# Eight LayerNorm tiles of a transformer block turned by DMA instead of by TensorE

## The chip, the cores and the metric

The kernel runs on one core of one Trainium2 chip. The metric is the device time of one execution in microseconds. The kernel before the change took 1726.68 us as the median of three runs, which lay between 1725.7 and 1727.48 us.

## The reference

One block with adaptive LayerNorm: attention over cached keys and values, then a gated feed-forward network (FFN). There are 2048 rows of width 512, 32 query heads and 8 key/value heads of width 128, a window of the last W = 512 keys, and F = 1792.

```python
mod = (_silu(c) @ w_mod).reshape(c.shape[0], 6, 1, -1)
sa, ca, ga, sb, cb, gb = (mod[:, 0], mod[:, 1], mod[:, 2], mod[:, 3], mod[:, 4], mod[:, 5])
h = _layernorm(x, axis=-1) * (1 + ca) + sa
x = x + ga * _A_ref(h, A_k_cache, A_v_cache, A_wq, A_wo)    # q = h@wq; softmax(q k^T / sqrt(128)) v; @wo
h = _layernorm(x, axis=-1) * (1 + cb) + sb
x = x + gb * _B_ref(h, B_w_gate, B_w_up, B_w_down)          # (gelu(h@w_gate) * (h@w_up)) @ w_down
return x
```

All inputs and the output are float32.

## The kernel before

**Arithmetic.** Products keep float32 accuracy with 16-bit matmuls: each factor is split into a high and a low fp16 half, and `mm3` (L87, its matmuls recorded at L91) makes three matmuls of every product. The projections use schemes with seven block products in place of eight (tiles `b`, `t`, `s`, `u`, `x`, and PSUM tiles `qa`, `qb`, `qc`).

**Order of the work.** The rows are worked in two halves of 1024. Attention makes 512 score tiles of 128 queries by 512 keys. One pass of the loop at L1581 is one **tick**, and it emits the instructions of every engine in the order in which the engine will run them:

- `scores(t)` (L989): three matmuls into PSUM tile `ps`. There are only two `ps` banks, so `scores(t+2)` has to wait until `ee` of tick t has been read from its bank.
- `peak(t)` (L998): VectorE takes the negated row maximum `nm` (L1000). `expo(t)` (L1003): ScalarE makes `ee` = exp(ps + nm) (L1009).
- `high(t-2)` (L1019): ScalarE writes the fp16 high half `p` (L1021). `low(t-3)` (L1024): VectorE writes the low half (L1026), and SyncE (SP) issues a DMA transpose of both halves into `pt` (L1030).
- Three tasks from a list for TensorE: PV products `po`, output projection `py`, query projection of later units (`qa`, `qb`, `qc`).
- The planned steps of this tick: first `run(t)`, then loads, then `run(("w", t))`.

All DMAs that matter here are issued by SP in program order (L97 records plain ones). ScalarE (ACT), VectorE (DVE) and GpSimd (POOL) also run strictly in program order, so a waiting instruction holds up all that stands behind it. Work that is planned with `sched` gets a load into the `raw` ring of five buffers, at a tick that a small planner (L1509) takes from the tick at which the buffer's last holder ends.

**The part that is changed.** While the first half's attention runs, the second half's first LayerNorm is made: `plan_gen(1, ...)` (L1211) lays eight tiles of 128 rows, one per 16 ticks, beginning at ticks 78, 94, ... 190. `ln_tile` (L490) gives the steps of one tile, at these ticks after its begin:

- `load`: DMA of 128 rows of x into a `raw` buffer, here called `xs`.
- `stat` (+0, L502): mean and variance on DVE, then a power on POOL (`rs`, L404). `norm` (+3, L506): DVE subtracts the mean and scales, in place (L509).
- `turn` (+5, L511): four TensorE transposes of 128x128 float32 into one PSUM bank `pln` (L514).
- `affine` (+6 and +7, L516): four ScalarE instructions read `pln`, apply scale and shift per feature, and write `hf` (L522). A DMA then keeps `hf` in DRAM (`hs`).
- `parts` (+8 and +9, L527): ScalarE makes fp16 high halves `b` (L534), POOL the low halves (L536). Tiles 0 to 3 make two blocks, tiles 4 to 7 one.

A third set of such tiles (generation 2, later) uses the same function and stays as it is. Where ticks 186 to 190 make `wo` weights, POOL runs four sets of three instructions (`raw`, `wo`, `wo`; L663, L161, L162) in a row, and behind them the chain `lw`, `lu`, `lt` of the next weight's scale (L237, L241, L263), for which DVE's reciprocal `lr` (L267) waits.

**A model for the new instructions.** At the end of the FFN the kernel already turns float32 tiles by DMA: `yt_turn` (L1728) has ScalarE part the 16-bit halves of each word (`yu`, L1733) and SP issue a DMA transpose (`yv`, L1738); `yt_row` joins the halves on ScalarE (L1757) or POOL (L1753).

Of the kernel before, what the change touches and what calls it, by code (L numbers as in the profile page):

```python
# [12 lines left out]
U16 = mybir.dt.uint16  # L13
BF16 = mybir.dt.bfloat16
AF = mybir.ActivationFunctionType
# [3 lines left out]
P = 128  # L19
S, D, F = 2048, 512, 1792  # L20
HQ, HKV, DH = 32, 8, 128
W = 512
KT = D // P
# [3 lines left out]
QT = QB // P  # L27
# [15 lines left out]
NOT = 12  # L43
# [10 lines left out]
NE = 6  # L54
# [5 lines left out]
SETPOS = (20, 14, 13, 12, 10, 8)  # L60
SETPOS2 = (18, 12, 11, 10, 9, 7)
TAIL = 12


@with_exitstack
def block_kernel(ctx: ExitStack, tc: tile.TileContext, x, kT, v, wq, wo, wg, wu, wd, cT, wc, wm, out):
    nc = tc.nc

    const = ctx.enter_context(tc.tile_pool(name="const", bufs=1))
    pool = ctx.enter_context(tc.tile_pool(name="pool", bufs=2))  # L70
# [7 lines left out]
    def raw(name):  # L78
        return pool.tile([P, 512], F32, tag="raw", name=name, bufs=NRAW)
# [4 lines left out]
    def bank(tag, name, bufs):  # L84
        return psum.tile([P, 512], F32, tag=tag, name=name, bufs=bufs)
# [9 lines left out]
    def dma(out_, in_):  # L95
        moved[0] += 1
        nc.sync.dma_start(out_, in_)  # L97
# [5 lines left out]
    def rows_of(t, i):  # L103
        return t[i * P:(i + 1) * P, :]
# [284 lines left out]
    def ln_cols(key):  # L389
        return (1, 0) if key == "a" else (4, 3)  # L390
# [12 lines left out]
    def ln_power(st):  # L403
        nc.gpsimd.tensor_tensor(st["rs"], st["rs"], nhalf, op=ALU.pow)  # L404
# [85 lines left out]
    def ln_tile(gen, i, src):  # L490
        jsc, jsh = ln_cols("a" if gen < 2 else "f")
        qb, i = divmod(i % (2 * QT), QT)
        st = {}

        def load():
            if gen == 2:
                st["x"] = src()
            else:
                st["x"] = raw("xs")
                dma(st["x"], src())  # L500

        def stat():  # L502
            ln_stat(st["x"], st)
            ln_power(st)

        def norm():  # L506
            if gen == 2:
                return pool_ts(st["x"], st["x"], st["mv"][:, 0:1], st["rs"], ALU.subtract, ALU.mult)
            nc.vector.tensor_scalar(st["x"], st["x"], st["mv"][:, 0:1], st["rs"], op0=ALU.subtract, op1=ALU.mult)  # L509

        def turn():  # L511
            st["ps"] = bank("acc", "pln", NACC)
            for dt in range(KT):
                nc.tensor.transpose(st["ps"][:, dt * P:(dt + 1) * P], st["x"][:, dt * P:(dt + 1) * P], ident)  # L514

        def affine(dts):  # L516
            if 0 in dts:
                st["f"] = raw("hf") if gen == 2 else tmp("hf")
            f = st["f"]
            for dt in dts:  # L520
                sl = slice(dt * P, (dt + 1) * P)
                nc.scalar.activation(f[:, sl], st["ps"][:, sl], AF.Identity,  # L522
                                     scale=cols[:, jsc, dt:dt + 1], bias=cols[:, jsh, dt:dt + 1])
            if KT - 1 in dts:
                dma(spilled(gen, qb)[:, :, i * P:(i + 1) * P], f.rearrange("p (k q) -> p k q", k=KT))

        def parts(act):  # L527
            o = slice(i * P, (i + 1) * P)
            f = st["f"].rearrange("p (k q) -> p k q", k=KT)
            for h, name in enumerate(("b11", "b21") if qb == 0 else (None, "b22")):  # L530
                if name:
                    t, src = block(gen, name), f[:, 2 * h:2 * h + 2, :]
                    if act:
                        nc.scalar.activation(t[:, 0:2, o], src, AF.Copy)  # L534
                    else:
                        nc.gpsimd.tensor_tensor(t[:, 2:4, o], src, t[:, 0:2, o], op=ALU.subtract)  # L536

        more = [lambda: parts(True), lambda: parts(False)]
        return load, [stat, norm, turn, lambda: affine((0, 1)), lambda: affine((2, 3))] + more

    TURN = {}

# [79 lines left out]
    def sched(pos, ld, *more, kind="raw", ahead=AHEAD):  # L622
        loads.append(((pos,) + more, ld, kind, ahead))
# [121 lines left out]
    def at(key, *fns):  # L745
        later.setdefault(key, []).extend(fns)
# [464 lines left out]
    def plan_gen(gen, t_ln, t_cb, dcb, src):  # L1211
        for i in range(2 * QT):
            t = t_ln[i]
            load, steps = ln_tile(gen, i, lambda i=i: src(i))
            sched(t, (load, steps[:3]), t + 3, t + 5)
            for off, fn in zip((6, 7, 8, 9), steps[3:]):
                at(("w", t + off), fn)
        for p in range(2):
            sched_combos(gen, p, t_cb + dcb * p)

    plan_gen(1, [78 + 16 * i for i in range(8)], 201, 33, lambda i: rows_of(x, 2 * QT + i))
    for p in range(2):
        sched_combos(2, p, 478 + 10 * p)

# [10 lines left out]
    for g in range(NG):  # L1235
# [6 lines left out]
        if 0 < g < GW:  # L1242
            a, b = plain_steps(g, by)
            sched_pair(g, srcs, t0 - (19 if g > 1 else 13), spread, [(t0 - (12 if g > 1 else 8), a)], [(t0 - (8 if g > 1 else 7), b)])
        elif g >= GW and (not half or pr < GW):
            sched_set(g, srcs, t0, by, spread)
            if not half:
                a, b, c, d, e, f = SETPOS2 if g == GW else SETPOS
# [11 lines left out]
        else:  # L1260
            if g > 0:
                if pr % 2 == 0:
                    load, stat, spread_, parts = k_items(pr)
                    sched(t0 - (22 if g > 2 else 20), (load, [stat]))
                    at(("w", t0 - (19 if g > 2 else 17)), spread_)
                load, stat, spread_, parts = k_items(pr)
                sched(t0 - (7 if g > 2 else 4 if g > 1 else 6), (load, [parts if g != 2 else lambda parts=parts: soon(parts(True))]))
                at(t0 - (3 if g > 2 else 1 if g > 1 else 2), lambda pr=pr: store(("k", pr), KV[0, pr, 0]))
                if pr % 2 == 0:
                    load, stat, spread_, parts = v_items(qd)  # L1270
# [221 lines left out]
    for n in range(NP):  # L1492
        b = T // 2 + 30 + 27 * n
# [84 lines left out]
    with tc.manual_schedule():  # L1578
        begin()
        nexty, invs = [], {}  # L1580
        for t in range(T + TAIL):  # L1581
            now[0] = t
            u, s = divmod(t, 4)
# [83 lines left out]
    for i, q in enumerate((16, 19, 22, 26, 30, 33, 36, 40)):  # L1667
        load, norm, split, turn = ln_turned(i)
# [192 lines left out]
```

## Time and profile before

| | |
|---|---|
| median of the runs | 1726.68 us (1725.7 to 1727.48) |
| span of the profiled execution | 1724.3 us |
| PE (TensorE) busy | 1705.4 us, 99% |
| DVE busy | 1424.2 us, 83% |
| ACT busy | 1257.4 us, 73% |
| POOL busy | 1088.1 us, 63% |
| chain that ended last | PE 92%, ACT 4%, DVE 2%, DMA 2% |

The page gives one time for the profiled execution, its span; it lies 2.4 us below the median of the runs. Busy is the time in which an engine ran at least one instruction. The chain that ended last is followed backwards from the last instruction through whatever each one waited for. The clock that TensorE was granted shows 9 tenths or more in each of the 40 slices of the page.

### The profile page before, as it was taken

The page shows a single profiled execution, that of the slowest core. Times are in us where ns is not written, and L with a number is a line of the kernel's source. Part 1 is how long each engine was busy: PE and PEld are TensorE (multiplying, and loading weights), DVE is VectorE, ACT ScalarE, POOL GpSimd, SP SyncE. Part 2 cuts the span into 40 slices and gives each one's busy share as a digit, 9 for nine tenths or more (in the row PEclk, how much of TensorE's full clock was granted, in tenths as well). Part 3 has the DMA queues.
Part 4 walks back from the last instruction along what each step waited for, and adds up shares of the span by engine and source line. Part 5 has one row for each costly group of instructions (what it writes and reads, how often), then busy time and mean ns, then how long its engine had stood idle before and what let it go on. Part 6 is the DMA issues. An engine that isn't in the chain of part 4 may idle for free.

```text
span 1724.3 us, 26250 instructions
## 1 busy us (share of the span) xinstructions
PE 1705.4 (99%) x7961; PEld 780.0 (45%) x7961; DVE 1424.2 (83%) x2480; ACT 1257.4 (73%) x2823; POOL 1088.1 (63%) x1322
## 2 busy tenths in 40 slices
PE   7999999999999999999999999999999999999999
PEld 4344444444444444444444444444444444444444
DVE  8888888888888999888888888888896788676666
ACT  7988788888878877888778777788785354455442
POOL 3879777776788884655665755757760345735424
PEclk9999999999999999999999999999999999999999
DMA  7999999999999998999999999899997556365353
GB/s 242 222 207 214 214 217 205 226 202 227 213 217 236 201 212 181 212 211 225 216 220 222 211 227 206 198 236 212 222 232 162 164 144 195 121 165 174 99 158 102
DMA packets 693454, 343.51 MB, mean 199 GB/s; under 512 B 579136, under 2 KB 602688, under 8 KB 693312
## 3 DMA queue, kind: packets, MB, share of 16 engines
q1 hardware_dynamic: 693024, 341.30, 85.3%
q8 instruction: 63, 1.03, 0.3%
q14 instruction: 79, 0.65, 0.1%
q10 hardware_dynamic: 288, 0.52, 0.1%
HBM read 137.50 MB, written 63.70 MB: 117 GB/s over the span
## 4 chain that ended last, share of the span: by engine, by line
PE 92%; ACT 4%; DVE 2%; DMA 2%; issue 1%; SPq 0%; ACTq 0%; DVEq 0%
PE py L91 20%; PE po L91 18%; PE ps L91 17%; PE fa L91 8%; PE qa L91 8%; PE fc L91 4%; PE qc L91 4%; PE ya L91 4%; PE qb L91 2%; PE fb L91 2%; PE yc L91 2%; ACT ee L1009 1%; ACT p L1021 1%; PE yb L91 1%; DMA rw<-in_wq 1%
## 5 line engine op out<-in xcount | busy, mean ns | idle before, releaser
L1009 ACT ACTIVATE ee<-ps,nm 128x512 f32<-128x512 f32 x512 | 349.7, 683 | 185.3 <-DVE nm L1000 182.7
L1026 DVE SCALAR_TENSOR_TENSOR p<-ee,rr,p 128x512 f16<-128x512 f32 x512 | 454.4, 888 | 8.5 <-ACT p L1021 8.0
L1000 DVE TENSOR_REDUCE nm<-ps 128x1 f32<-128x512 f32 x512 | 350.1, 684 | 96.8 <-PE ps L91 94.9
L91 PE MATMUL ps<-k,qt 128*128 128x512 f16 x1536 | 414.7, 379 | 4.4 <-ACT ee L1009 3.3
L1021 ACT ACTIVATE p<-ee,rr 128x512 f16<-128x512 f32 x512 | 363.9, 711 | 16.5 <-DVE rr L1017 11.8
L91 PE MATMUL po<-pt,v 128*128 128x512 f16 x1536 | 372.9, 379 | 2.1 <-DMA pt<-p 0.8
L91 PE MATMUL py<-wo,ot 128*128 128x512 f16 x1536 | 371.3, 379 | 0.0
L91 PEld LDWEIGHTS <-w 128*128 128x128 f16 x2184 | 213.4, 98 | 259.6 <-issue 2.0
L91 PEld LDWEIGHTS <-v 128*128 128x128 f16 x1536 | 149.8, 98 | 184.6 <-issue 3.0
L91 PEld LDWEIGHTS <-ot 128*128 128x128 f16 x1536 | 150.3, 98 | 181.2
L91 PEld LDWEIGHTS <-qt 128*128 128x128 f16 x1536 | 145.7, 98 | 178.0 <-issue 6.0
L1337 POOL TENSOR_TENSOR fg<-fg 128x512 f32<-128x512 f32 x48 | 62.9, 1311 | 135.8 <-DVE fg L1311 133.0
L754 DVE SCALAR_TENSOR_TENSOR ot<-po,ot 128x512 f16<-128x512 f32 x128 | 87.8, 686 | 40.4 <-ACT ot L753 39.9
L1321 ACT ACTIVATE at<-fg 128x512 f16<-128x512 f32 x92 | 56.3, 626 | 77.8 <-DVE fg L1311 61.0
L1009 ACT ACTIVATION_READ_ACCUMULATOR ee<-ps,nm 128x1 f32 x512 | 100.1, 196 | 0.0
L970 DVE SCALAR_TENSOR_TENSOR acc<-py,ysc,acc 128x512 f32<-128x512 f32 x128 | 94.7, 739 | 5.3 <-PE py L91 5.3
L91 PE MATMUL qa<-t,w 128*128 128x512 f16 x348 | 84.9, 379 | 0.0
L91 PE MATMUL fa<-t,w 128*128 128x512 f16 x336 | 81.7, 379 | 0.1
L237 POOL TENSOR_TENSOR lw<-lw,half__86 128x1 f32<-128x1 f32 x38 | 25.9, 681 | 85.7 <-DVE lw L188 85.6
L753 ACT ACTIVATE ot<-po 128x512 f16<-128x512 f32 x128 | 73.9, 578 | 5.0 <-PE po L91 5.0
L404 POOL TENSOR_TENSOR rs<-rs,nhalf 128x1 f32<-128x1 f32 x32 | 18.5, 577 | 93.7 <-DVE rs L398 85.8
L91 PEld LDWEIGHTS <-wo 128*128 128x128 f16 x504 | 49.3, 98 | 59.7 <-issue 0.5
(258 smaller groups left out, 2802.9 us busy)
## 6 DMA issues: line engine op xcount, KB each, us to landing
w<-kept SPq DMA_DIRECT2D x123, 256.0 KB, 3.3
wo<-kept SPq DMA_DIRECT2D x72, 256.0 KB, 3.2
kept<-stage SPq DMA_DIRECT2D x67, 256.0 KB, 3.0
raw<-in_wo SPq DMA_DIRECT2D x56, 256.0 KB, 3.2
kept<-w SPq DMA_DIRECT2D x39, 256.0 KB, 3.0
rw<-in_wq SPq DMA_DIRECT2D x38, 256.0 KB, 3.1
hs<-hf SPq DMA_DIRECT2D x32, 256.0 KB, 2.9
pt<-p SPq DMA_TRANSPOSE x512, 3.4
```

Of the source, the lines that this page charges most:

```text
L91: nc.tensor.matmul(ps, a, b, start=first and n == 0, stop=last and n == 2, skip_group_check=chain)
L237: nc.gpsimd.tensor_tensor(out, out, half_, op=ALU.pow)
L404: nc.gpsimd.tensor_tensor(st["rs"], st["rs"], nhalf, op=ALU.pow)
L753: nc.scalar.activation(t[:, 0, :], src, AF.Copy, scale=scale)
L754: return lambda: nc.vector.scalar_tensor_tensor(t[:, 1, :], src, scale, t[:, 0, :], op0=ALU.mult, op1=ALU.subtract)
L970: nc.vector.scalar_tensor_tensor(acc[ti], st["p"], by, acc[ti], op0=ALU.mult, op1=ALU.add)
L1000: nc.vector.tensor_reduce(nm, E[t]["ps"], axis=AX.X, op=ALU.max, negate=True)
L1009: nc.scalar.activation(e, E[t]["ps"], AF.Exp, bias=E[t]["nm"], scale=1.0, accum_out=sm[:, t % 2:t % 2 + 1])
L1021: nc.scalar.activation(p16[:, 0, :], E[t]["e"], AF.Copy, scale=E[t]["r"])
L1026: nc.vector.scalar_tensor_tensor(p16[:, 1, :], E[t]["e"], E[t]["r"], p16[:, 0, :], op0=ALU.mult, op1=ALU.subtract)
L1321: nc.scalar.activation(t[:, 0, :], g, AF.Copy)
L1337: nc.gpsimd.tensor_tensor(g[o], g[a], g[b], op=ALU.subtract)
```

## The change

For generation 1 (`TG = (1,)`) `turn` is replaced by three steps, and all steps of a tile move into the planner's list, so that the `raw` buffer is held from load to the last step:

- `split` (+4): ScalarE copies `xs` as 16-bit words into `xu`, high halves and low halves apart.
- `spin` (+5): SP issues one DMA transpose of the 128x1024 16-bit words into `xt`.
- `join` (+7): ScalarE interleaves the halves back into the `raw` buffer `xs`, which is float32 again, now turned.
- `affine` (all four at +10) works in place on `xs` in SBUF; there is no `hf` and no PSUM bank.
- `parts` at +11 (ScalarE) and +12 (POOL). Tile 2 and tile 6 begin two ticks later than before, tile 7 one earlier.

```diff
--- before.py
+++ after.py
@@ -60,6 +60,7 @@
 SETPOS = (20, 14, 13, 12, 10, 8)
 SETPOS2 = (18, 12, 11, 10, 9, 7)
 TAIL = 12
+TG = (1,)
 
 
 @with_exitstack
@@ -513,8 +514,21 @@
             for dt in range(KT):
                 nc.tensor.transpose(st["ps"][:, dt * P:(dt + 1) * P], st["x"][:, dt * P:(dt + 1) * P], ident)
 
+        def split():
+            st["u"] = pool.tile([P, 2, W], U16, tag="e", name="xu", bufs=NE)
+            nc.scalar.activation(st["u"], st["x"].bitcast(U16).rearrange("p (r h) -> p h r", h=2), AF.Copy)
+
+        def spin():
+            st["t"] = pool.tile([P, 2 * KT, P], U16, tag="ot", name="xt", bufs=NOT)
+            nc.sync.dma_start_transpose(st["t"], st.pop("u").rearrange("p a b -> p (a b)"))
+
+        def join():
+            a, b = st["x"].bitcast(U16).rearrange("p (q h) -> p h q", h=2), st.pop("t").rearrange("p (h k) q -> p h (k q)", h=2)
+            nc.scalar.activation(a, b, AF.Copy)
+            st["f"] = st["ps"] = st["x"]
+
         def affine(dts):
-            if 0 in dts:
+            if 0 in dts and "f" not in st:
                 st["f"] = raw("hf") if gen == 2 else tmp("hf")
             f = st["f"]
             for dt in dts:
@@ -536,7 +550,7 @@
                         nc.gpsimd.tensor_tensor(t[:, 2:4, o], src, t[:, 0:2, o], op=ALU.subtract)
 
         more = [lambda: parts(True), lambda: parts(False)]
-        return load, [stat, norm, turn, lambda: affine((0, 1)), lambda: affine((2, 3))] + more
+        return load, [stat, norm] + ([split, spin, join] if gen in TG else [turn]) + [lambda: affine((0, 1)), lambda: affine((2, 3))] + more
 
     TURN = {}
 
@@ -1212,13 +1226,11 @@
         for i in range(2 * QT):
             t = t_ln[i]
             load, steps = ln_tile(gen, i, lambda i=i: src(i))
-            sched(t, (load, steps[:3]), t + 3, t + 5)
-            for off, fn in zip((6, 7, 8, 9), steps[3:]):
-                at(("w", t + off), fn)
+            sched(t, (load, steps[:9]), *[t + off for off in (3, 4, 5, 7, 10, 10, 11, 12)])
         for p in range(2):
             sched_combos(gen, p, t_cb + dcb * p)
 
-    plan_gen(1, [78 + 16 * i for i in range(8)], 201, 33, lambda i: rows_of(x, 2 * QT + i))
+    plan_gen(1, [78 + 16 * i + (0, 0, 2, 0, 0, 0, 2, -1)[i] for i in range(8)], 201, 33, lambda i: rows_of(x, 2 * QT + i))
     for p in range(2):
         sched_combos(2, p, 478 + 10 * p)
```

What moves, by engine. On TensorE 32 transposes go and every other row keeps its place.

**ScalarE, around the first tile.** `junk` belongs to another tensor's spread of values. Before:

```order
324 L220 ACTIVATE junk,lm<-raw 128x512
325 L1009 ACTIVATE ee,sm<-ps,nm 128x512
326 L1021 ACTIVATE p_3082<-ee,rr 128x512
327 L522 ACTIVATE hf<-pln,cols 128x128 x2
328 L1009 ACTIVATE ee,sm<-ps,nm 128x512
329 L1014 ACTIVATE rr<-sm 128x2
330 L1021 ACTIVATE p_3116<-ee,rr 128x512
331 L753 ACTIVATE qt<-qd,qsc 128x512
332 L522 ACTIVATE hf<-pln,cols 128x128 x2
333 L1009 ACTIVATE ee,sm<-ps,nm 128x512
334 L1021 ACTIVATE p_3147<-ee,rr 128x512
335 L903 ACTIVATE s_3156<-qa 128x512
```

With the change, the same stretch at three places (`split`, `join`, `affine`):

```order
319 L519 ACTIVATE xu<-xs 128x1024
320 L221 ACTIVATE junk,lm<-raw 128x512
321 L1023 ACTIVATE ee,sm<-ps,nm 128x512
322 L1028 ACTIVATE rr<-sm 128x2
323 L1035 ACTIVATE p_3052<-ee,rr 128x512
324 L767 ACTIVATE ot<-po 128x512
```

```order
329 L1028 ACTIVATE rr<-sm 128x2
330 L1035 ACTIVATE p_3112<-ee,rr 128x512
331 L767 ACTIVATE qt<-qd,qsc 128x512
332 L527 ACTIVATE xs<-xt 128x2x512
333 L1023 ACTIVATE ee,sm<-ps,nm 128x512
334 L1035 ACTIVATE p_3140<-ee,rr 128x512
```

```order
340 L1023 ACTIVATE ee,sm<-ps,nm 128x512
341 L1035 ACTIVATE p_3209<-ee,rr 128x512
342 L536 ACTIVATE xs<-xs,cols 128x128 x4
343 L1023 ACTIVATE ee,sm<-ps,nm 128x512
344 L1028 ACTIVATE rr<-sm 128x2
```

The split stands ahead of a `junk`; the join stands where the second pair of `affine` stood; the four `affine` instructions stand together, three score tiles later, ahead of one `ee`.

**SP, around the first tile.** Before:

```order
178 L1030 DMA_TRANSPOSE pt<-p_3019 128x8x128
179 L97 DMA kept<-wo 128x1024
180 L1030 DMA_TRANSPOSE pt<-p_3050 128x8x128
181 L97 DMA kept<-wo 128x1024
182 L1030 DMA_TRANSPOSE pt<-p_3082 128x8x128
183 L97 DMA hs_0_3131<-hf 512x1x128
```

With the change:

```order
178 L1044 DMA_TRANSPOSE pt<-p_3019 128x8x128
179 L523 DMA_TRANSPOSE xt<-xu 128x8x128
180 L98 DMA kept<-wo 128x1024
181 L1044 DMA_TRANSPOSE pt<-p_3052 128x8x128
182 L98 DMA kept<-wo 128x1024
```

The new transpose goes in directly behind one `pt` transpose and ahead of a plain DMA; the write of `hs` follows later.

**POOL, around ticks 186 to 194.** `b` is the low half of tile 6 (its row before stands 18 rows earlier, at 456); `rs` is tile 7's. Before:

```order
474 L663 TENSOR_TENSOR raw<-raw,gs 128x512
475 L161 TENSOR_SCALAR wo<-raw 128x512
476 L162 TENSOR_TENSOR wo<-raw,wo 128x512
477 L663 TENSOR_TENSOR raw<-raw,gs 128x512
478 L161 TENSOR_SCALAR wo<-raw 128x512
479 L162 TENSOR_TENSOR wo<-raw,wo 128x512
480 L404 TENSOR_TENSOR rs<-rs,nhalf 128x1
481 L237 TENSOR_TENSOR lw<-lw,half__86 128x1
482 L241 TENSOR_SCALAR lw<-lw 128x1
```

With the change:

```order
468 L162 TENSOR_SCALAR wo<-raw 128x512
469 L163 TENSOR_TENSOR wo<-raw,wo 128x512
470 L550 TENSOR_TENSOR b_5426<-xs,b_5426 128x2x128
471 L677 TENSOR_TENSOR raw<-raw,gs 128x512
472 L162 TENSOR_SCALAR wo<-raw 128x512
473 L163 TENSOR_TENSOR wo<-raw,wo 128x512
474 L677 TENSOR_TENSOR raw<-raw,gs 128x512
475 L162 TENSOR_SCALAR wo<-raw 128x512
476 L163 TENSOR_TENSOR wo<-raw,wo 128x512
477 L405 TENSOR_TENSOR rs<-rs,nhalf 128x1
478 L677 TENSOR_TENSOR raw<-raw,gs 128x512
479 L162 TENSOR_SCALAR wo<-raw 128x512
```

Tile 6's `b` now stands among the four `wo` sets, so it lies between them and the `lw` chain behind them; tile 7's `rs` moves ahead of the fourth set.

## Rows read from the trace of the kernel before

**Rows 1.** Busy time by stretch: PE, PEld, DVE, ACT, POOL (instructions), clock, DMA share, GB/s.
```profile
220.00:300.00 80.00, 80.00 (x381) 36.87 (x379) 71.05 (x130) 67.47 (x165) 60.49 (x81) 1.00 0.95 215
...
400.00:520.00 120.00, 120.00 (x571) 55.26 (x570) 103.59 (x190) 97.27 (x235) 94.78 (x123) 1.00 0.97 213
```

**Rows 2.** Chain of waits between 200 and 560 us, by line.
```profile
by line: PE ps L91 25.7%; PE py L91 25.6%; PE po L91 25.5%; PE qa L91 12.6%; PE qc L91 6.5%; PE qb L91 3.2%; PE pln L514 1.0%; PE pst L224 0.0%
```

**Rows 3.** Timeline of PE around the first tile's transposes: start, us, instruction.
```profile
230.66 0.60 PE L514 MATMUL pln<-ident,xs 128*128 128x128 f32 x4
231.10 0.81 PE L91 MATMUL ps<-k,qt 128*128 128x512 f16 x3
...
241.49 0.81 PE L91 MATMUL ps<-k,qt 128*128 128x512 f16 x3
```

**Rows 4.** Tile pln: count, ns min/median/max, first and last start.
```profile
L514 PE MATMUL pln<-ident,xs x32: 272/273/273, 230.7 to 515.5; 128*128 128x128 f32 x32
```

**Rows 5.** Timeline of ACT in the same place (idle before it, and its releaser, in brackets).
```profile
231.24 0.69 ACT L1009 ACTIVATE ee<-ps,nm 128x512 f32<-128x512 f32 x1 [0.41 <-DVE nm L1000]
...
237.93 0.79 ACT L522 ACTIVATE hf<-pln,cols 128x128 f32<-128x128 f32 x2
238.61 0.69 ACT L1009 ACTIVATE ee<-ps,nm 128x512 f32<-128x512 f32 x1
```

**Rows 6.** Groups by line and shape, whole span: busy us, mean ns, idle before, releaser.
```profile
L1733 ACT ACTIVATE yu<-yt 128x1024 uint16<-128x1024 uint16 x16 | 16.5, 1046 | 0.9 <-DVE yt L1707 0.9
...
L1757 ACT ACTIVATE yr<-yv 128x1024 uint16<-128x1024 uint16 x8 | 9.0, 1164 | 1.0 <-DMA out_y<-yr 1.0
...
L553 ACT ACTIVATE xs<-xs,kinv,kmax 128x512 f32<-128x512 f32 x8 | 6.4, 801 | 0.0
...
L448 ACT ACTIVATE hf<-pln,cols 128x512 f32<-128x512 f32 x4 | 2.8, 769 | 0.0
```

**Rows 7.** Groups by line and shape between 220 and 540 us.
```profile
L1009 ACT ACTIVATE ee<-ps,nm 128x512 f32<-128x512 f32 x125 | 85.4, 683 | 41.3 <-DVE nm L1000 40.2 <-POOL w L162 0.4
```

**Rows 8.** Tile pt: issue on SP's queue, who waited for it, landing after issue.
```profile
L1030 SPq DMA_TRANSPOSE pt<-p x512: 1231/1234/3518, 35.5 to 1323.0; - x171
...
  PE po L91: 0.8, 1
...
DMA to landing us min/median/max: 3.0/3.4/6.5
```

**Rows 9.** SP's queue around the first tile's turn.
```profile
233.53 1.29 SPq L1030 DMA_TRANSPOSE pt<-p  x1
234.88 0.57 SPq L97 DMA_DIRECT2D kept<-wo  x1
```

**Rows 10.** Timeline of POOL, 485 to 516 us.
```profile
485.33 1.12 POOL L536 TENSOR_TENSOR b<-hf,b 128x256 f16<-128x256 f32 x1
486.54 0.23 POOL L241 TENSOR_SCALAR ysc<-ysc 128x1 f32<-128x1 f32 x1
...
515.19 0.60 POOL L241 TENSOR_SCALAR lt<-lt 128x1 f32<-128x1 f32 x1
```

**Rows 11.** Timeline of DVE, 515 to 517 us.
```profile
515.82 0.16 DVE L267 RECIPROCAL lr<-lt 128x1 f32<-128x1 f32 x1
...
516.55 0.68 DVE L1000 TENSOR_REDUCE nm<-ps 128x1 f32<-128x512 f32 x1
```

**Rows 12.** Timeline of ACT, 517 and 529 us.
```profile
517.27 0.69 ACT L1009 ACTIVATE ee<-ps,nm 128x512 f32<-128x512 f32 x1 [1.47 <-DVE nm L1000]
...
529.04 0.68 ACT L1009 ACTIVATE ee<-ps,nm 128x512 f32<-128x512 f32 x1
```

**Rows 13.** Timeline of PE, 518 and 531 us.
```profile
518.21 0.81 PE L91 MATMUL ps<-k,qt 128*128 128x512 f16 x3
...
531.16 0.81 PE L91 MATMUL ps<-k,qt 128*128 128x512 f16 x3
```

**Rows 14.** Timeline of PE, 730 to 770 us: waits of over 0.15 us before a score matmul.
```profile
734.36 0.81 PE L91 MATMUL ps<-k,qt 128*128 128x512 f16 x3 [0.19 <-ACT ee L1009]
...
763.76 0.81 PE L91 MATMUL ps<-k,qt 128*128 128x512 f16 x3 [0.16 <-ACT ee L1009]
```

## The prediction

> **What bounds the kernel now.** I read the busy time by stretch first: in the part of the program that the change touches, PE is busy for the whole of each stretch (80.00 of 80 us, 120.00 of 120) at a granted clock of 1.00, while ACT is busy for 84 and 81% of them [rows 1]. The chain of waits through 200 to 560 us then shows what ends last: PE's own instructions and nothing else, the transposes `pln` with 1.0% among them [rows 2]. So in this part the time is the sum of what PE is given to do. An instruction that leaves PE gives back its own length; one that is added elsewhere costs nothing until it makes PE wait.
>
> **What the change takes from PE.** The four transposes of the first tile start at 230.66 us and the score matmuls behind them at 231.10 [rows 3]: 0.44 us. The row of the tile gives 273 ns for one transpose [rows 4], but that is a duration, and pipelined matmuls overlap; what counts is start to start, 0.11 us each. There are 32 transposes [rows 4], in eight tiles: 8 × 0.44 = **3.5 us**. The chain says the same: 1.0% of 360 us is 3.6. Nothing else leaves PE and nothing is added.
>
> At this place the Trainium skill speaks against the change. The page "VectorE: DVE Perf Modes", section "The three transpose paths", gives 390 ns for a 128x128 transpose on TensorE and 1309 ns on the DMA path (for 16-bit data, of which our float32 tile has twice as many blocks), and its "Rules for kernel authors" advise TensorE wherever a PSUM destination is fine. By its 390 ns the 32 transposes would be worth 12.5 us, by the trace 3.5: the measurement decides. Its rule compares two times in isolation; what it would do here is the slow rival below.
>
> **What it adds to ACT.** For each tile ACT gets a split and a join. The same two operations on the same 128x1024 words exist at the end of the program: 1046 ns and 1164 ns [rows 6], together 2.2 us, 17.7 us in eight tiles. The `affine` instructions are as many as before but read SBUF instead of PSUM. A scaled copy of 128x512 takes 801 ns from SBUF and 769 from PSUM [rows 6], so I change nothing for that (4% of 1.4 us a tile). Against this stands ACT's idle time: 41.3 us between 220 and 540 us ahead of `ee` alone, nearly all of it waiting for DVE's `nm` [rows 7]. In sum it fits more than twice over; the question is whether it fits where it lands.
>
> What lands late does harm like this: `ee` of tick t frees the bank of `scores(t+2)`, and if `ee` ends later than that matmul's start, PE stands. At the first tile, `ee` runs from 238.61 for 0.69 us, to 239.30 [rows 5], and the score matmul that needs its bank starts at 241.49 [rows 3]: 2.19 us of cover. With the 0.44 us of transposes gone PE comes that much earlier against what it waits for; I count 1.75.
> - The split stands ahead of a `junk` and an `ee` that had 0.41 us of wait [rows 5]; of its 1.05 us some 0.6 stay. Hidden.
> - The join takes the place of a pair of `affine` (237.93 to 238.61, 0.68 us [rows 5]): 1.16 − 0.68 = 0.48 us later. Hidden, if its data is there.
> - Four `affine` at one place: 2 × 0.68 = 1.36 us ahead of one `ee`. Hidden with 0.4 us to spare; if they met a place with less cover they would cost what is missing. Bounds 0 to 1 us in all.
>
> **What it adds to SP and the DMA.** Each tile adds one DMA transpose of 128x8x128 words: the very form of `pt`, of which there are 512, 1.23 us of SP's queue each and 3.4 us from issue to landing [rows 8]. SP passes it between a `pt` and a plain load, so the next `pt` issues some 1.25 us later. The 512 `pt` have made PE wait 0.8 us in the whole program, once [rows 8]; a `pt` 1.25 us later in one of 16 ticks I put at 0 (at most 8 × 0.44 again, if each ate its own gain). The join waits for the landing: the transpose can issue where `kept` did, at 234.88 [rows 9], and lands 3.4 us later at 238.3, 0.35 us after the join could have begun (237.93). With the 0.48 that is 0.83 of the 1.75 us of cover. Hidden.
>
> **Where cover is thin.** Around 515 us POOL runs four `wo` sets on end, then the chain up to `lt`, which starts at 515.19 and lasts 0.60 [rows 10]; DVE's `lr` starts just then, at 515.82, and `nm` behind it at 516.55 [rows 11]. The `ee` that waited for this `nm` runs 517.27 to 517.96 [rows 12]; the matmul that needs its bank starts at 518.21 [rows 13]. Cover: 0.25 us, less the 0.44 of tile 7's transposes, which lie in between: −0.19. And the change moves the low half `b` of tile 6 in ahead of this chain: 485.33 to 486.54, 1.2 us in its old place [rows 10], 0.9 as I take it for the mean between a free and a shared run (estimate; bounds 0.6 to 1.2). So PE waits 0.9 + 0.19 = **1.1 us** here once (0 if POOL catches up on waits that I don't see, 1.4 at the long `b`). Behind it, tile 7's four `affine` now precede the `ee` of 529.04 to 529.72 [rows 12], whose bank is needed at 531.16 [rows 13]: 1.44 − 1.36, next to nothing; I take **0.2 us** (0 to 0.5).
>
> **Sum.** −3.5 + 1.1 + 0.2 = −2.2 us. The profiled execution has a span of 1724.3 us, which makes 1722.1; it lies 2.4 us below the median of the runs, so against that median 1726.7 − 2.2 = **1724.5 us**. Its own range comes from the bounds: 1723.2 (neither wait) to 1725.6 (1.4 + 0.5 and some 0.5 elsewhere). A measurement here can tell a change of about 0.2%, 3.45 us, from none. The whole of what PE gives back, 3.5 us, is just that much.
>
> **Rivals.**
> - *All of it stays hidden* (chance 0.22). POOL's sets may run shorter than I add, since DVE no longer stands for tile 7's `rs`. For it speaks that PE hardly waits anywhere in this part [rows 1]. Time: 1723.2; two later waits of PE for `ee`, 0.19 and 0.16 us [rows 14], may close as well: 1722.8. Against it: a cover of 0.25 us.
> - *More places like the thin one* (0.15). The `wo` sets, K blocks and new steps come round every 16 ticks; if the other six tiles lose 0.25 to 0.5 us each to late `pt`, late loads or a late `b`, that is 1.5 to 3 us more: 1726.0 to 1727.5. Against it: the cover of 2.19 us at the first tile.
> - *The join waits for its DMA and ACT stands* (0.10), slower. The join sits in ACT's program order ahead of an `ee`. If the landing takes L, ACT is late by L − 3.05 (237.93 − 234.88) + 0.48, and PE waits for what exceeds 1.75: it decides at L = 4.3 us. The `pt` row's longest is 6.5 [rows 8]: 2.2 us for that tile. If half of the eight met that, 4 × 2.2 = 8.8 us, and 1726.7 − 3.5 + 8.8 = 1732.0. For it speaks a DMA share of 0.95 to 0.97 in this part [rows 1], against it the median of 3.4 under that same share, 512 times. This is what the skill's rule, "Use TensorE if PSUM dest is OK", would come to here: the slower path lands on a queue that matters.
> - That the change does not do what it says is out: 32 transposes are gone from PE's rows, with no others in their place.
>
> **How the numbers follow.** The forecast has 0.53, the rivals 0.22, 0.15 and 0.10. Predicted is the likeliest, 1724.5. The range holds the first three, from 1722.6 to 1727.5: 0.9 less the tails of each, about 0.83. Faster by over 0.2% means below 1723.2: the hidden case sits on that line and below, most of its 0.22, and a little of the forecast, 0.24 together. Slower by over 0.2%, above 1730.1, is the DMA case: 0.08. The rest, 0.68, is within 0.2%.
>
> **What would show it.** Right: no row `pln<-ident,xs` on PE; `xu` near 1.05 us, `xs<-xt` near 1.16 us, `xt` landing near 3.4 us after issue; PE still busy for the whole of 220 to 500 us; and by about 520 us every score matmul some 2 us earlier than now, against 3.5 if all was hidden. The lost part should show as one wait of PE for `ee`, itself behind DVE's `nm` and `lr`, near 515 us. Wrong: ACT's join with an idle time ahead of it that is put down to `xt` and, behind it, PE waiting for `ee` tile after tile (slow rival); PE waits for `po<-pt` (SP too late); a chain in which DVE or ACT takes more than a per cent of 220 to 540 us.

## The result, and the profile after

| | before | after |
|---|---|---|
| median of 21 runs each | 1726.77 us (1725.31 to 1728.98) | 1730.16 us (1726.89 to 1732.35) |
| ratio, 95% interval | | 1.0016 (1.0010 to 1.0023) |
| span of the profiled execution | 1724.3 us | 1729.3 us |
| ACT busy | 1257.4 us | 1274.3 us |

The change is slower: by 0.16% (2.8 us) by the ratio, and by 3.4 us by the two medians. The measured 1730.16 us lies outside the range that I gave (1722.6 to 1727.5) and on the other side of no change from the forecast. The profiled execution of after took 1731.07 us, some 0.9 more than its median.

The busy time by stretch, after (columns as in [rows 1]): PE is no longer busy throughout, and its clock falls in one place.

```profile
300.00:400.00 100.00, 99.24 (x466) 44.95 (x464) 87.89 (x163) 89.91 (x214) 76.21 (x104) 1.00 1.03 225
400.00:520.00 120.00, 116.14 (x539) 52.29 (x538) 106.43 (x188) 102.13 (x239) 92.89 (x121) 0.99 1.00 222
...
514.00:518.00 4.00, 1.65 (x8) 0.68 (x7) 2.88 (x8) 3.97 (x10) 3.52 (x8) 1.00 1.01 228
518.00:522.00 4.00, 3.83 (x11) 1.36 (x11) 3.17 (x8) 3.51 (x11) 3.73 (x6) 0.57 0.87 192
```

The chain of waits from 200 to 560 us, by line. Before it was PE alone [rows 2]; now ACT, DVE and POOL have pieces of it.

```profile
by line: PE po L92 19.1%; PE ps L92 18.7%; PE py L92 17.6%; PE qa L92 9.4%; PE qc L92 5.0%; ACT ee L1023 3.6%; DVE p L1040 2.7%; ACT p L1035 2.5%; PE qb L92 2.5%; issue 2.3%; DVE nm L1014 2.2%; ACT qt L767 1.6%; DVE qt L768 1.3%; POOL raw L
```

What PE waited for from 200 to 560 us (us in total, times, longest):

```profile
PE qa L92 <- ACT u L917: 2.1, 3, 1.2
PE pst L225 <- ACT junk L221: 1.5, 1, 1.5
PE ps L92 <- ACT ee L1023: 1.0, 2, 0.5
```

To see where time went, I subtract the start of each tick's score matmul in the trace of before from the one after, and list the ticks where the difference steps:

```
tick    before    after   difference   what lies just ahead
 32      99.64    99.98      +0.33     the start of the program
 84     231.10   231.00      -0.10     -0.44, transposes of tile 0 gone
100     271.76   271.22      -0.54     -0.44, tile 1
116     312.39   311.56      -0.83     -0.44, tile 2 (+0.15 at tick 104)
130     348.70   348.79      +0.09     +0.92, qa waits for u in tick 129
148     393.68   392.89      -0.78     -0.44 twice, tiles 3 and 4
162     429.99   429.54      -0.44     +0.34, qa waits for u in tick 161
180     474.96   473.65      -1.32     -0.44 twice, tiles 5 and 6
194     511.28   511.28      +0.01     +1.32, qa waits for u in tick 193
195     513.86   514.52      +0.66     +0.65, ps waits for ee
196     515.62   518.17      +2.55     +1.89 with tile 7's -0.44 in it: pst waits for junk, ps for ee
197     518.21   522.41      +4.20     +1.65, matmuls at the lower clock
358     927.55   932.22      +4.67     +0.51, then +0.41
511                          +4.96     end of the span
```

The gain is there, tile by tile: eight times 0.44 us. It is lost in ticks 129, 161 and 193 to 196: 0.92 + 0.34 + 1.32 + 0.65 + 2.33 (1.89 and the 0.44 hidden in it) + 1.65 = 7.2 us. (In the table a tick's loss shows in the start of the next one.) With 0.15 at tick 104, 7.4 − 3.5 = 3.9 us for these ticks, near the 3.4 of the medians. Steps of up to 0.5 us at the start and after tick 358 come in other kernels too (below) and are not explained here.

### The profile page after: what moved, and what is told of

Same layout as the page of the kernel before. It is cut to its first block, busy times and chain, and to the rows that moved or that the text cites. A ratio compares the mean times of both kernels' runs of the same rounds, so it can differ in the third digit from the quotient of the medians.

```text
span 1729.3 us, 26241 instructions
## 1 busy us (share of the span) xinstructions
PE 1703.7 (99%) x7928; PEld 775.8 (45%) x7929; DVE 1428.1 (83%) x2480; ACT 1274.3 (74%) x2839; POOL 1088.5 (63%) x1322
## 4 chain that ended last, share of the span: by engine, by line
PE 84%; ACT 7%; DVE 5%; DMA 2%; POOL 1%; issue 1%; SPq 0%; POOLq 0%; ACTq 0%; DVEq 0%
PE py L92 18%; PE po L92 16%; PE ps L92 16%; PE fa L92 8%; PE qa L92 8%; PE fc L92 4%; PE qc L92 4%; PE ya L92 3%; PE fb L92 2%; PE qb L92 2%; ACT ee L1023 2%; PE yc L92 2%; ACT p L1035 1%; DVE p L1040 1%; DVE nm L1014 1%
## 5 line engine op out<-in xcount | busy, mean ns | idle before, releaser
L1040 DVE SCALAR_TENSOR_TENSOR p<-ee,rr,p 128x512 f16<-128x512 f32 x512 | 459.1, 897 | 9.6 <-ACT p L1035 9.2
L1719 DVE SCALAR_TENSOR_TENSOR yt<-ya,dyc,yt 128x512 f32<-128x512 f32 x82 | 60.3, 745 | 19.4 <-PE ya L92 19.4
```

The lines of the kernel that those rows point to most:

```text
L1040: nc.vector.scalar_tensor_tensor(p16[:, 1, :], E[t]["e"], E[t]["r"], p16[:, 0, :], op0=ALU.mult, op1=ALU.subtract)
L1719: nc.vector.scalar_tensor_tensor(YT[key], ps, by, YT[key], op0=ALU.mult, op1=ALU.add)
```

## The experiments

Theories: **A**, the raw buffer, held for 13 ticks instead of 6, makes loads late; **B**, the work added to ACT makes the waits; **C**, the moved low half on POOL does. Later ones: **D**, PE's lead (it comes earlier, since its transposes are gone) is lost at the next wait, whatever ACT does; **E**, the low half on POOL stretches DVE. All medians below stand beside runs of before taken with them, whose medians were 1726.5 to 1727.05 us. The intervals are 0.07 to 0.14% (1.2 to 2.4 us) either way, so two kernels less than some 2 us apart are not told apart by their times alone.

### Buffers of their own for the turned tiles (own_ring, own_two, own_16)

```diff
-                st["x"] = raw("xs")
+                st["x"] = pool.tile([P, 512], F32, tag="xr", name="xs", bufs=NX) if gen == 1 else raw("xs")
...
-            sched(t, (load, steps[:9]), *[...])
+            sched(t, (load, steps[:9]), *[...], kind="xr" if gen == 1 else "raw")
```

NX is 1 in own_ring, 2 in the others. own_16 also has the tiles begin at 78 + 16i.

> The change, but its tiles lie in a buffer of their own, so that the five raw buffers serve the other loads alone; all steps at the same ticks. Theory A (a raw buffer that is held for 13 ticks instead of 6 makes four loads come only in the tick that uses them, at ticks 89, 122, 153 and 186; POOL, DVE and ACT then run late and PE waits at ticks 129, 161, 193 to 196): POOL's waits of 4.7 us for raw<-in_wo go, PE's waits at these ticks mostly go, 1723.5 to 1725.0 us. Theory B (the split, the join and the four affine in a row make ACT late by themselves): the waits stay, 1728.5 us or more. Theory C (the low half of tile 6 among the wo sets): the waits at 129 and 161 go, those at 193 to 196 stay, about 1728.

Measured: 1734.02 us, ratio 1.0040 (1.0026 to 1.0054). One buffer was a bad choice of mine: a tile's load now waited for the tile before, its statistics on DVE waited for the load, and PE lost 4.2 us at tick 192 and 1.5 at 129. So with two:

> As own_ring, but with two buffers of their own, so that a tile's load no longer waits for the tile before and its statistics on DVE don't wait for the load (which made PE wait 4.2 us at tick 192 and 1.5 at 129). Theory A: 1723.5 to 1726 us. Theory B: 1728 to 1731 us, with waits of PE for u at ticks 16k+1 left.

Measured: 1727.65 us, 1.0005 (0.9996 to 1.0014): 2.5 us less than the change (the two intervals overlap a little), and between what A and B had promised. The traces show that the held buffer is what makes loads late: POOL stands five times ahead of its `raw` rows in the change, 11.4 us in all between 200 and 560 us, and never in own_two, as in before. By the planner's rule (L1509) the loads of `wo` for ticks 122 and 186 get the buffers of tiles 2 and 6, which the change frees only after ticks 124 and 188, so they are issued in the very tick that uses them. The timeline of POOL near tick 186, after:

```profile
493.34 0.69 POOL L242 TENSOR_SCALAR gs<-gate,osc 128x512 f32<-128x512 f32 x1 [0.73 <-DVE osc L289]
498.74 1.28 POOL L677 TENSOR_TENSOR raw<-raw,gs 128x512 f32<-128x512 f32 x1 [4.70 <-DMA raw<-in_wo]
```

This `raw` row began at 495.27 before; the whole chain of `wo` sets, and `lw` and `lr` behind it, moved back with it ([rows 10, 11]: `lr` at 515.82, now 517.59).

> As own_two, but all tiles begin at 78 + 16i as before the change, so that tile 7's split no longer stands ahead of the ACT instruction (junk) that PE's pst waited for, 1.4 and 0.6 us, at tick 195. If that place is what is left of the loss beside the waits for u: the wait for junk goes, 1725.5 to 1727 us, against 1727.65 of own_two. If the split does its harm wherever it stands: 1727.5 or more.

Measured: 1726.93 us, 0.9999 (0.9990 to 1.0008). The wait for `junk` is gone, and the kernel is level with before. Most of what is left of the loss is one kind of wait, at ticks 97, 129, 161 and 193, after which PE's starts step back by 0.6 to 0.7 us each, 2.5 us in all; smaller steps near ticks 95 and 120 to 127 make 1.2 more (PE's waits from 200 to 560 us):

```profile
PE qa L93 <- ACT u L918: 1.9, 4, 0.5
PE ps L93 <- ACT ee L1024: 0.3, 1, 0.3
```

### The held buffer without the added work, and the work without the buffer

hold_only keeps TensorE's transposes, one tick ahead of the affine, and has the other steps at the ticks of the change and its held buffers:

```diff
-TG = (1,)
+TG = ()
...
-            if 0 in dts and "f" not in st:
-                st["f"] = raw("hf") if gen == 2 else tmp("hf")
+            if 0 in dts:
+                st["f"] = raw("hf") if gen == 2 else st["x"]
...
-            sched(t, (load, steps[:9]), *[t + off for off in (3, 4, 5, 7, 10, 10, 11, 12)])
+            sched(t, (load, steps[:7]), *[t + off for off in (3, 9, 10, 10, 11, 12)])
```

> TensorE transposes the eight tiles as before (one tick ahead of the affine), and there is no split, transpose by DMA or join; but the tiles begin at the ticks of the change, the affine writes into the raw buffer and this is held for 13 ticks. Theory A: the losses of the change without its gain, 1728.5 to 1733 us. Theory B: 1726.1 to 1727.5 us, as before the change. Theory C: losses near tick 193 alone, about 1729.

Measured: 1728.31 us, 1.0010 (1.0002 to 1.0019): 1.75 us slower than before, most of the losses near tick 195 (0.36, 0.94 and 0.44 us in the starts of ticks 195, 196 and 199). This does not part A from C, which expected about 1729 here, and the four affine in a row are in it too. extra_work is the kernel before, with a split, a DMA transpose and a join into a scratch tile added to each tile (the code of `split` and `spin` of the change, and):

```diff
+        def join():
+            j = pool.tile([P, 512], F32, tag="xj", name="xj", bufs=1)
+            a, b = j.bitcast(U16).rearrange("p (q h) -> p h q", h=2), st.pop("t").rearrange(...)
+            nc.scalar.activation(a, b, AF.Copy)
```

> The kernel before with TensorE's transposes, plus the split, the DMA transpose and the join of each tile at the same offsets as in the change, the join into a scratch tile that nobody reads; raw buffers held for 6 ticks as before. Theory A: 1726.5 to 1728 us, the added 17.7 us of ACT and 8 transposes are hidden. Theory B: 1729.5 to 1734 us. Theory C: as A.

Measured: 1731.08 us, 1.0026 (1.0016 to 1.0035). So the split, the DMA transpose and the join, which I had called hidden, cost 4.5 us by themselves, with no buffer held longer, nothing moved on POOL and nothing taken from PE. **A and C as the only cause fall; B holds.** The place is mostly not `ee` but `u`, in ticks 97, 113, 129, 161 and 193 (PE's waits from 200 to 560 us):

```profile
PE qa L91 <- ACT u L916: 2.2, 5, 0.5
PE ps L91 <- ACT ee L1022: 0.2, 1, 0.2
```

### Taking the added work out piece by piece

no_turn is the kernel before without transposes and without anything in their place; no_act is the change without split, DMA and join; no_spin without the DMA alone; no_join without the join alone. In each, a step's body is emptied:

The edit of no_turn, in `turn` of the kernel before:

```diff
+            if gen == 1:
+                st["ps"] = st["x"]
+                return
```

The three that go in no_act; the first of them alone goes in no_spin (its join reads `st.pop("u")`), the last alone in no_join:

```diff
-            nc.sync.dma_start_transpose(st["t"], st.pop("u").rearrange("p a b -> p (a b)"))
...
-            nc.scalar.activation(st["u"], st["x"].bitcast(U16).rearrange("p (r h) -> p h r", h=2), AF.Copy)
...
-            nc.scalar.activation(a, b, AF.Copy)
```

> The kernel before without the 32 transposes and with nothing in their place: the affine reads the unturned tile from its raw buffer (held two ticks longer), so the second half's result is not the reference's. Theory P (what leaves PE is gained, if nothing is added): 1723.0 to 1724.0 us. Theory D (in the ticks 16k+1 the query projection's matmul qa waits for ACT's copy u, with some 0.5 us to spare before; PE comes 0.44 us earlier per tile and loses it at the next such place, since DVE and ACT don't come earlier): 1725.0 to 1727.0 us, with PE waiting for u at ticks 97, 113 and so on.

> The change without split, transpose by DMA and join (the tile stays unturned, so the second half's result is not the reference's); buffers, ticks, affine and parts as in the change. Theory B (ACT's 2.2 us per tile makes the loss): 1724 to 1726.5 us. Theory A (the held buffer alone): 1728.5 us or more, as the change.

> The change with split and join on ACT but without the DMA transpose between them (the join reads the split's tile, so the tile stays unturned and the second half's result is not the reference's). Theory B: 1729 to 1731 us, as the change. If SP's queue or the landing of the transposed tile makes the loss: 1725 to 1727.5 us.

> The change without the join (split and DMA transpose stay, the turned tile is read by nobody, the affine reads the unturned tile, so the second half's result is not the reference's). If the loss goes with ACT's amount of work, about half of what split, join and transpose cost together (4.5 us, from the change to no_act) goes with the join: 1727.3 to 1728.5 us. If the split ahead of junk and u does all the harm: 1729.5 or more.

| kernel | median, us | ratio to before, 95% |
|---|---|---|
| no_turn | 1724.08 | 0.9986 (0.9978 to 0.9995) |
| no_act | 1725.61 | 0.9994 (0.9985 to 1.0003) |
| no_join | 1726.64 | 1.0003 (0.9994 to 1.0012) |
| no_spin | 1728.32 | 1.0009 (1.0000 to 1.0018) |
| the change | 1730.16 | 1.0016 (1.0010 to 1.0023) |

no_turn sets what there is to win: 2.5 us (0.9 to 3.8 by its interval), and up to tick 196 its trace keeps all eight steps of 0.44 with no wait for `u`. So D falls for `u`: PE's lead alone does not lose its gain there. It does lose some behind: in the trace of no_turn some 2 us go between ticks 196 and 359, beside waits for `ee` at ticks 197 (0.16) and 213 (0.55).

Taking ACT's work and the DMA out of the change wins 4.55 us back (no_act); the join alone 3.5, the DMA alone 1.8, by the medians. By the ratios it is 0.22, 0.13 and 0.07% (3.8, 2.2 and 1.2 us), and the DMA's part is not clear of the noise; no_spin fell between its two expectations. The parts need not add up, since they share the same places. The late loads alone do not make the waits for `u`: no_act holds the buffers as the change does, POOL stands 4.1 and 3.7 us ahead of the same two `raw` rows (4.7 each in the change), and PE never waits for `u`. Added from the other side the parts do come near: −2.5 (no_turn) + 4.5 (extra_work) + 1.75 (hold_only) = 3.75 us, against 3.4 measured.

A rival was not run by itself: `xu` and `xt` take buffers from the rings that `ee` and `ot` use. In the trace of after no wait of ACT between 200 and 560 us is put down to such a buffer, and no_join, which still takes both, has no wait for `u`.

Without the join, the waits for `u` are gone and those near 515 us stay (PE's waits from 200 to 560 us, no_join):

```profile
PE pst L225 <- ACT junk L221: 1.5, 1, 1.5
PE ps L92 <- ACT ee L1021: 1.2, 2, 0.7
```

How does a join in tick 119 (tile 2) make `u` late in tick 129? Here is how long after a tick's first score matmul its `ee` starts, taken from the starts in the three traces:

```
tick       119   120   121   122   123   124   125   126   127   128   129
before    2.23  1.62  1.58  1.62  1.62  2.62  2.42  1.96  1.97  1.84  1.58
no_join   2.86  2.25  1.84  1.57  3.25  3.27  3.04  2.60  3.04  2.91  2.03
after     2.87  3.47  2.14  2.13  4.24  4.25  4.19  3.74  4.13  4.00  3.13
```

The join makes `ee` 1.2 us later in tick 120. In tick 123 the next blow falls: the four `affine` of the tile, in one row on ACT directly ahead of the `ee` (ACT, after):

```profile
332.41 1.64 ACT L536 ACTIVATE xs<-xs,cols 128x128 f32<-128x128 f32 x4
333.95 0.67 ACT L1023 ACTIVATE ee<-ps,nm 128x512 f32<-128x512 f32 x1
```

From there the lag of some 4 us stays for six ticks. ACT first runs on without a pause to 342.6 us; the high half of `b` and two `junk` fall into this stretch. Then `ee` waits for DVE's `nm`, and `nm` stands in DVE's queue behind low halves that are long beside POOL's late `wo` set (which starts at 336.63 us, after 4.70 us of waiting for `in_wo`) or wait for ACT. `u` stands in the same ACT queue. PE's `qa` writes the one bank that `u` reads; in before `u` ended 1.28 us ahead of it in this tick (PE and ACT, after):

```profile
345.28 0.81 PE L92 MATMUL ps<-k,qt 128*128 128x512 f16 x3
346.85 1.46 PE L92 MATMUL qa<-t,x 128*128 128x512 f16 x6 [0.76 <-ACT u L917]
```

```profile
344.20 0.69 ACT L1023 ACTIVATE ee<-ps,nm 128x512 f32<-128x512 f32 x1 [1.60 <-DVE nm L1014]
...
345.12 0.71 ACT L1035 ACTIVATE p<-ee,rr 128x512 f16<-128x512 f32 x1
345.73 0.58 ACT L767 ACTIVATE ot<-po 128x512 f16<-128x512 f32 x1
346.21 0.59 ACT L917 ACTIVATE u<-qa 128x512 f32<-128x512 f32 x1
```

### Other ticks for the same steps (short_hold, moved_steps, own_early, own_earliest)

Each changes only the offsets (of norm, split, DMA, join, two pairs of affine, two parts); the last three have the two buffers of own_two and tiles that begin at 78 + 16i, in moved_steps at 62 + 16i.

For short_hold the edit is

```diff
-            sched(t, (load, steps[:9]), *[t + off for off in (3, 4, 5, 7, 10, 10, 11, 12)])
+            sched(t, (load, steps[:9]), *[t + off for off in (3, 4, 5, 7, 8, 8, 9, 10)])
```

and the others have (3, 4, 5, 10, 12, 13, 16, 20) in moved_steps, (3, 4, 5, 7, 8, 8, 9, 9) in own_early and (3, 4, 4, 6, 6, 7, 8, 9) in own_earliest.

> The change with the affine at +8 and the parts at +9 and +10, so that the raw buffer is held for 11 ticks in place of 13. Theory A: loads come up to two ticks less late, part of the losses goes, 1725.5 to 1728.5 us. Theory B: no gain, 1729.5 or more, since the affine comes a tick after the join.

> Two buffers of their own, tiles begin one period earlier (62 + 16i), and the steps stand in the ticks of a period in which ACT idles ahead of ee in the trace of before: split +4, DMA +5, join +10, affine in two pairs at +12 and +13, high half at +16, low half on POOL at +20, where POOL idles 2.6 us. Theory B refined (not the amount of ACT's added work but the ticks it falls in; the cover is at u and junk, not at ee): PE keeps most of the 3.5 us, as in no_turn, 1723.5 to 1725.5 us, no wait for u of more than 0.3 us. If the amount itself is too much: 1727 or more.

> As own_16 (two buffers of their own, tiles at 78 + 16i), with all four affine at +8 and both halves of the parts at +9, so that POOL's low half runs ahead of the wo sets as before the change, not next to them. Theory E (what remains of the loss at ticks 16k+1 comes from the moved low half on POOL, which stretches DVE's p and so delays nm, ee and u): waits for u of 0.6 us at ticks 97, 129, 161 and 193 go, 1724 to 1726 us. Theory B (ACT's added 2.2 us per tile): waits stay, 1727 or more.

> As own_early, but with the DMA transpose at +4, join and one pair of affine at +6, the other pair at +7, and the parts at +8 and +9, the ticks they had before the change: only the split and the join are added to ACT's order of before. Theory E: 1724 to 1726 us. Theory B: 1727 or more. If the join now waits for the landing of its tile, ACT shows idle time put down to xt, and PE waits for ee at ticks 16k+6 to 16k+8: 1727 to 1730 us.

Measured: 1733.95, 1730.61, 1734.07 and 1733.23 us (ratios 1.0043, 1.0024, 1.0041 and 1.0040, no interval reaching below 1.0015). All four are worse than own_16, and every expectation of a gain failed. Theory E falls with own_early: the low half ran early and PE still waited for `u`, 3.7 us in seven ticks. Closer steps bring new waits for `ee` as well. In own_earliest, the waits from 200 to 700 us of PE and of ACT for the transposed tile were:

```profile
PE ps L93 <- ACT ee L1024: 4.9, 4, 1.6
...
ACT xs L528 <- DMA xt<-xu: 3.6, 4, 1.1
...
PE qa L93 <- ACT u L918: 2.7, 6, 0.5
```

moved_steps was laid out by ACT's idle time per tick, and waited for `u` in seven ticks: idle time ahead of an `ee` is time in which ACT waits for DVE, and work put there can delay DVE's next input all the same.

### Only the odd tiles

In own_16 the waits came 19 ticks after the begin of tiles 0, 2, 4 and 6 and not of 1, 3 and 5.

```diff
-([split, spin, join] if gen in TG else [turn])
+([split, spin, join] if gen in TG and odd else [turn])
```

> As own_16, but only tiles 1, 3, 5 and 7 are turned by DMA; tiles 0, 2, 4 and 6 by TensorE, with their steps as before the change. In own_16 PE waited 0.6 us for u at ticks 97, 129, 161 and 193, each 19 ticks after the begin of tiles 0, 2, 4 and 6, and not at 113, 145 and 177. If each tile's own work on ACT makes the wait behind it: these waits go and 4 x 0.44 us are kept, 1724.5 to 1725.7 us. If PE's lead makes them, whatever ACT did: 1726 to 1727.5 us, with waits for u left.

Measured: 1725.90 us, 0.9994 (0.9985 to 1.0002). The time lies between the two ranges; the trace decides. No wait for `u` is left between 200 and 560 us, and the four steps of 0.44 stay until tick 196. Then 0.3 us go at tick 197 and 1.0 at tick 206, where `po` waits for DVE's `kmax`:

```profile
PE po L93 <- DVE kmax L188: 0.9, 1, 0.9
PE ps L93 <- ACT ee L1025: 0.2, 1, 0.2
```

So each tile's own steps (split, DMA and join, with the later affine and parts) make the wait behind it. This is the best version that computes the whole; it beats the change (1725.9 against 1730.2), but against before its interval holds no change.

## Why the prediction was wrong, point by point

- **What leaves PE: right in the size, not in what it is worth.** 0.44 us a tile, eight times, stands in the trace of after as forecast. But no_turn, with nothing in place of the transposes, gained 2.5 us by the median and not clearly all 3.5, since PE then met other waits.
- **The split, the join and the four affine "hidden": the step that failed.** I set each against the 2.19 us of cover that one `ee` of the first tile had, one at a time. Three things were wrong in it. The cover of `ee` is not the least one: `qa` needs `u`, and `pst` needs a `junk`, and I had looked at neither. Second, delays add: what the join leaves is not drained before the four `affine` come, three ticks on. Third, ACT's 41.3 us of idle [rows 7] was no reserve: it is time in which ACT waits for DVE, and moved_steps, which put the work there, still lost 4.1 us. extra_work prices split, DMA and join at 4.5 us, where I had written nought.

  The `u` of tick 97 in the timeline of ACT, before, and its `qa` in that of PE, before: it ends at 264.91, and `qa` begins 0.56 us later. Over the ticks 81 to 193 this time to spare is 0.5 to 1.3 us, in ticks 129, 161 and 193 1.2 to 1.3.

```profile
264.33 0.58 ACT L903 ACTIVATE u<-qa 128x512 f32<-128x512 f32 x1
```

```profile
265.47 1.46 PE L91 MATMUL qa<-t,x 128*128 128x512 f16 x6
```

- **Durations.** `xu` took 1047 ns, as forecast; the join 1353, not 1164 [rows 6]; the landing of `xt` had the median 3.4 us of `pt` [rows 8], up to 5.6. From the views of tile `xt` (issue, join, who waited, landing), after:

```profile
L523 SPq DMA_TRANSPOSE xt<-xu x8: 1277/1336/1896, 235.3 to 518.8; - x8
L527 ACT ACTIVATE xs<-xt x8: 1342/1353/1367, 239.0 to 522.6; 128x1024 uint16<-128x1024 uint16 x8
...
  DMA xt<-xu: 2.3, 3
...
DMA to landing us min/median/max: 3.1/3.4/5.6
```

- **The added wait in front of the join: small.** ACT stood 2.3 us for `xt` in all, in three of eight tiles, 1.3 at most. That was tile 1, whose transpose landed after 5.6 us, past the 4.3 from which the slow rival has PE wait 1.3 us; PE lost 0.15 there (tick 104). The slow rival had the right sign and not the right mechanism: no_spin, whose join waits for no DMA, still has 1.9 us of waits for `u`, against 2.1, so the join harms mostly by its length.
- **The raw buffer: no term in the sum.** Late loads stand only in the rival "more places", which came nearest to what happened, at 0.25 to 0.5 us a place. I had not asked which later loads get the buffer that is held. Two of them start POOL's `wo` sets 4.7 us late. The held buffer, with the steps at their new ticks, costs 1.75 us (hold_only).
- **The thin place near 515 us: right place, wrong size and wrong wait.** I gave it 1.3 us; it cost 4.6 (0.65 + 2.33 + 1.65), after 1.32 for `u` just ahead of it. The wait that I forecast, `ee` behind `nm` and `lr`, is not among PE's: this `lr` starts at 517.59, its `ee` at 519.03, and the score matmul that needs the bank only at 522.41, since PE had stood by then for other reasons. Nor did the 0.2 us at 529 come. What PE waited for first is an `ee` whose `nm` stood behind tile 7's `norm` (DVE, 511.58 for 1.48 us); then the split of tile 7, which stands ahead of the `junk` that `pst` waits for and of the next `ee`. hold_only and no_act, which have no split, wait 0.6 us for this `junk`, so some 0.9 of the 1.53 are the split's; own_16, with tile 7 a tick later, has no such wait (ACT, then PE, after):

```profile
515.80 1.04 ACT L519 ACTIVATE xu<-xs 128x1024 uint16<-128x1024 uint16 x1
516.75 0.62 ACT L221 ACTIVATE junk<-raw 128x512 f16<-128x512 f32 x1
```

```profile
517.51 0.16 PE L225 MATMUL pst<-lm,ones 128*128 128x1 bf16 x1 [1.53 <-ACT junk L221]
518.17 1.44 PE L92 MATMUL ps<-k,qt 128*128 128x512 f16 x3 [0.50 <-ACT ee L1023]
519.40 2.52 PE L92 MATMUL qc<-t,w 128*128 128x512 f16 x6
```

- **The rule that spoke against it.** The Trainium skill ("VectorE: DVE Perf Modes", "Rules for kernel authors") advises TensorE for a 128x128 transpose when PSUM will do. The runs agree with it for this kernel, but not by the 0.39 us of the page's "The three transpose paths": PE paid 0.11 us a transpose, start to start. The DMA by itself is priced at 1.2 to 1.8 us in all eight tiles (no_spin), which is not clear of the noise. What weighed most was ACT's work for the split and the join of a float32 tile.

Open: that PE waits behind the even tiles and not the odd ones is seen in own_16 but not explained; a tile's stretch has other work in odd and even periods, and I did not part it. It does not hold everywhere: extra_work waits at tick 113 too, behind tile 1, and own_early at 113, 145 and 177. The steps of 0.3 to 0.9 us at the start and near tick 358, which differ between kernels, are open too.

## What to carry to other kernels

Before you call added work hidden, list every instruction on the bounding engine that waits for the engine you load, and take the shortest time to spare among them (here a copy with 0.56 us, not the exponential with 2.19). Then add the delays over all the ticks until the queue has run empty, instead of setting each against a fresh cover. A buffer that is held longer must be followed to the next loads that get it: the price falls on whoever uses those.

## What the runs showed of the hardware

After PE had stood for 1.5 and 0.5 us near 517 us, its granted clock was 0.57 in 518 to 522 us, so for most of it the lower of the two levels, 1.2 GHz in place of 2.4; the six `qc` matmuls took 2.52 us where six take 1.46 at the full clock (as in the `qa` row above), and three score matmuls 1.44 instead of 0.81 [rows 3]. It cost 1.65 us on top of the waits, and all stood at 1.00 again from 522. But such waits did not always bring it: in the same ticks PE stood 0.73, 1.52 and 0.50 us in no_join, and its clock stayed at 1.00 (columns as in [rows 1], no_join):

```profile
513.00:517.00 4.00, 1.98 (x10) 0.81 (x9) 3.41 (x8) 3.71 (x8) 3.34 (x10) 1.00 0.76 173
517.00:521.00 4.00, 4.00 (x20) 1.86 (x19) 3.17 (x8) 3.26 (x9) 3.75 (x5) 1.00 1.10 225
```

The same holds for no_spin and short_hold. Of the sixteen traces only own_ring has another such stretch between the start and the end of the program, behind a wait of 4.06 us. So the 1.65 us is shown for the one profiled execution of after, and not that the others paid it.

DVE's low half of `p` takes 0.73 us and up to 1.83 us. In the longest ones POOL runs an instruction with two input tensors for over a microsecond of it; DVE and POOL, after:

```profile
503.42 1.83 DVE L1040 SCALAR_TENSOR_TENSOR p<-ee,rr,p 128x512 f16<-128x512 f32 x1
```

```profile
503.43 1.27 POOL L677 TENSOR_TENSOR raw<-raw,gs 128x512 f32<-128x512 f32 x1
504.79 0.94 POOL L162 TENSOR_SCALAR wo<-raw 128x512 f16<-128x512 f32 x1
```

So a POOL instruction that moves by a microsecond may make a DVE one a microsecond longer. It does not always: 60 of the 381 low halves in the first 1000 us ran beside such a POOL instruction for over 0.5 us and stayed under 0.8. That both share something was not tried by itself.
